# One weighing of v for all eight batches of a gated attention and MLP kernel, with a rewritten instruction list

## The chip, the cores and the metric

The kernel runs on one core of a Trainium2 chip. The metric is the device time of one launch in microseconds; lower is better. All times here are microseconds (us) unless they are marked ns. The engines are TensorE (PE, with its weight loads as PEld), VectorE (DVE), ScalarE (ACT), GpSimd (POOL) and SyncE (SP, which issues DMAs).

## What is computed

Attention over 8 batches, 8 heads, 576 positions and 64 columns a head, with a causal mask and a gate `s` that adds a bias; then a layer norm and an MLP of 512 to 2048 to 512 columns with a residual. The reference, cut to what matters:

```python
scores = scale * np.matmul(q, k.transpose(0, 1, 3, 2))
cum = np.cumsum(np.maximum(s, 0.0), axis=-1)
bias = -(cum[:, :, :, None] - cum[:, :, None, :])
scores = np.where(causal, -1000000000.0, scores + np.minimum(bias, 0.0))
attn = np.exp(scores - np.max(scores, axis=-1, keepdims=True))
attn = attn / (np.sum(attn, axis=-1, keepdims=True) + 1e-09)
attn_out = np.matmul(attn, v)
...
xn = (x - mu) / np.sqrt(var + 1e-06) * g_ln
out = x + np.maximum(xn @ w_ch1, 0.0) @ w_ch2
```

Row i of the bias is -cum[i] + cum[j]. The term in i falls out of the division by the row's sum, so exp(cum[j]), taken relative to a constant, can be multiplied into row j of v and into the column of ones that gives the row's sum.

## The kernel before

A sequence of 576 positions is four tiles of 128 and a tail of 64. The work of a batch is: bring q and k of each head to columns by position (transposes), scores by key tile and exp of them, the causal mask, the product of exp with v and its column of ones, the division by the sums, the layer norm, and the MLP. The MLP of a batch is a queue of units: 16 units `h` of four 512-column products on w1 (`mlp1`, L758) and 16 units `y` of four on w2 (`mlp2`, L776). The eight tails of 64 rows are put in pairs into four more tiles at the end (`mixed_units`, L822).

Nothing is scheduled by a tool: every engine takes its instructions in the order in which the program issues them, and that order is written by hand as a list of words (`PLAN`, L1273), each of which calls one step (`STEPS`) and may name an engine (`:A` ACT, `:D` DVE, `:P` POOL). `u` and `U` take the next MLP unit from the queue, with its relu on ACT or DVE. What stands ahead of the list (loads, memsets) is in its order in the program. DMAs are issued by SP, ACT and POOL; those of POOL convert float32 to bf16 and stand in POOL's list between its own work.

There are three ways of attention in this kernel:

- Batch 0 goes by tiles. `ld_cast_tile` (L178) loads k and q of a tile; `tile_tr` (L939) transposes 8 heads' blocks in two groups `g` of four heads, `tile_evac` (L951) copies them out of PSUM, `tile_scores` (L961) makes scores and adds the causal mask by a product of `ident` with `maskT` (L974), `tile_exp` takes exp on ACT (L983), `tile_pv` (L1012) multiplies with v, `tile_norm` divides. The gate is part of the scores' products: q and k have 68 rows, 64 of data and four for the cumulative sum in three bf16 pieces. These come from a chain at the start: relu, scan (L292), pieces (L303 to L313), transposes of the pieces (`bias_tr`, L271) and copies into the rows of k and q (`bias_cols`, L280). Steps named `T`, `e`, `S`, `x`, `V`, `N` in the list.
- Batch 1 goes by heads: `tr_kind` (L317, six transposes for a pair of heads), `evac_half` (L329), `scores` (L382, one head of 68 rows, masks by a product for the first heads), `scores_d` (L420), `pv` (L573), `pv_norm`. The gate's rows come by SP's DMAs (`aug`, L261).
- Batches 2 to 7 go by pairs of heads: `burst` (L541) makes the scores of two heads at once, one in rows 0 to 63 and one in rows 64 to 127 of TensorE; `burst_exp` (L551); `burst_mask` (L560, POOL); `pv_two` (L613); `norm_two` (L639). The 64-row tails of the eight heads are one step (`tails`, L514). The gate is multiplied into v on POOL (`weigh_v`, L229) with `wt`, the exp of the cumulative sum (`sums_rel`, `sums_tr`, `sums_exp`, L1111 to L1130), and `weigh_ones` (L239) writes wt in two bf16 pieces into the two ones columns, four POOL steps a batch. Batch 2's q and k are loaded by pairs, copied to the side (`side_two`, L342), transposed (`tr_two`, L355) and copied out (`evac_two`); those of batches 3 to 7 are loaded as float32 rows by SP, cast by POOL (`cast_rows`) and transposed by DMA (`tr_rows`).

The early steps use four kinds of PSUM banks: `m` 2, `s` 3, `t` 2, `o` 1. The step `to` (`to_pairs`, L1096) closes these for `m` 2 and `s` 6. `keep_warm` (L851) makes products of zeros, nine at the start and three in the list.

Of the kernel before, what the change touches and what calls it, by code (L numbers as in the profile page):

```python
# [9 lines left out]
F32 = mybir.dt.float32  # L10
# [20 lines left out]
def fast_path(  # L31
# [24 lines left out]
    KA = D + 4  # L56
# [4 lines left out]
    NP = B * NJ  # L61
    NOLD = 2
    NPAIR = 3
    N0 = 12
    D2 = D + 2
    ET = H * TL + 2 * TL
    NM = 10
    KT = 96
# [12 lines left out]
    ps = ctx.enter_context(ExitStack())  # L81
    pool = {
        tag: ps.enter_context(
            tc.tile_pool(name="ps_" + tag, bufs=n, space=bass.MemoryType.PSUM)
        )
        for tag, n in (("m", 2), ("s", 3), ("t", 2), ("o", 1))
    }

    def ptile(tag, shape, name, dtype=F32):
        return pool[tag].tile(shape, dtype, name=name, tag=tag)  # L90
# [5 lines left out]
    maskT = const.tile([P, P], BF16, name="maskT")  # L96
# [8 lines left out]
    eight = hT[0:BH, 0, 0 : 2 * P].bitcast(F32)  # L105
# [6 lines left out]
    def home(gam):  # L112
        return 2 if gam == 2 else gam % 2

# [4 lines left out]
    rinvs = const.tile([P, B, H, NT], F32, name="rinvs")  # L119
    c_end = const.tile([BH, 1], F32, name="c_end")  # L120
# [4 lines left out]
    c3f = const.tile([P, 3 * S], BF16, name="c3")  # L125
    c3 = c3f[0:KT].rearrange("p (j s) -> p j s", j=3)
    ed = [c3f[:, i * ET : (i + 1) * ET] for i in range(2)]
    c_hi, c_mid, c_lo = (c3[0:BH, j, :] for j in range(3))
    zeros = hT[:, 1, :]

    rowb = const.tile([P, NT, 2 * H, KA], BF16, name="rowb")

    rows = [
        x[:, 0 : NT * 2 * H * D].rearrange("p (t u h d) -> p t u h d", t=NT, u=2, h=H)
        for x in (rowb.rearrange("p t h c -> p (t h c)"), kqf[2])
# [29 lines left out]
    def tile_dst(kind, t):  # L165
        pn = P if t < NF else TL
        u = "kq".index(kind)
        return rowb[0:pn, t, u * H : (u + 1) * H, 0:D]
# [16 lines left out]
    def ld_cast_pair(g):  # L185
        ld_cast("k", g)
        ld_cast("q", g)

    def ld_cast_v(b, t):
        pn = P if t < NF else TL  # L190
        nc.gpsimd.dma_start(
            out=v_bf[b % 2][:pn, t, :, 0:D],
            in_=v[b, :, t * P : t * P + pn, :].rearrange("h s d -> s h d"),
        )

# [5 lines left out]
    def ld_f32(kind, b, t):  # L201
        pn = pn_of(t)
        own = kind == "v" and "v" in pool
        tmp = (pool["v"] if own else stage).tile([P, H, D], F32, name="rowtmp", tag="st")
        nc.sync.dma_start(
            out=tmp[0:pn],
            in_=src_of[kind][b, :, t * P : t * P + pn, :].rearrange("h s d -> s h d"),
        )
        loaded[kind, b, t] = tmp

# [28 lines left out]
    def weigh_ones(b, eng="pool"):  # L239
# [21 lines left out]
    def aug(gam, eng, h0=0):  # L261
        r = slice(gam * G + h0, gam * G + G)
        i = home(gam)
        eng.dma_start(out=kq[i][D : D + 1, 1, h0:G, 0:S], in_=c_hi[r, :])
        for j in range(3):
            eng.dma_start(out=kq[i][D + 1 + j : D + 2 + j, 0, h0:G, 0:S], in_=c3[r, j, :])

    trc_bank = ptile("o", [P, 3 * NT * BH + KT - BH], "trc", BF16)
    trc = trc_bank[:, 0 : 3 * NT * BH].rearrange("p (t j x) -> p j t x", t=NT, j=3)

    def bias_tr(t):  # L271
        pn = P if t < NF else TL
        for j in range(3):
            o = (t * 3 + j) * BH
            nc.tensor.transpose(
                trc_bank[0:pn, o : o + KT], c3[:, j, t * P : t * P + pn], ident[0:KT, 0:KT]
            )


    def bias_cols(t0, t1, pn=P):  # L280
        nc.vector.tensor_copy(
            out=rowb[0:pn, t0:t1, 0:H, D + 1 : KA],
            in_=trc[0:pn, :, t0:t1, 0:H].rearrange("p j t x -> p t x j"),
        )
        nc.vector.tensor_copy(out=rowb[0:pn, t0:t1, H : 2 * H, D], in_=trc[0:pn, 0, t0:t1, 0:H])


    def sums_in(c0, c1):
        return (c_first if c1 <= 2 * P else c_in)[:, c0:c1]

    def cum_scan(c0, c1):
        nc.vector.tensor_tensor_scan(  # L292
            out=c_sc[:, c0:c1],
            data0=c_one[:, 0 : c1 - c0],
            data1=sums_in(c0, c1),
            initial=0.0 if c0 == 0 else c_sc[:, c0 - 1 : c0],
            op0=ALU.mult,
            op1=ALU.add,
        )

    def cum_cast(src, dst, c0, c1, eng):  # L303
        x, y = src(c0, c1), dst[:, c0:c1]
        if eng == "act":
            nc.scalar.copy(out=y, in_=x)
        else:
            nc.vector.tensor_tensor(out=y, in0=x, in1=x, op=ALU.max)

    def cum_rest(src, piece, dst, c0, c1):  # L310
        nc.vector.tensor_tensor(
            out=dst(c0, c1), in0=src(c0, c1), in1=piece[:, c0:c1], op=ALU.subtract
        )  # L313

    trs = {}

    def tr_kind(kind, g):  # L317
        src = ready.pop((kind, g))
        tr = ptile("t", [P, S], "trqk", BF16)
        for t in range(QT):  # L320

            nc.tensor.transpose(
                tr[:, t * QP : (t + 1) * QP],
                src[0:QP].rearrange("p h c -> p (h c)")[:, t * P : (t + 1) * P],
                ident[0:QP, 0:QP],
            )
        trs[kind, g] = tr

    def evac_half(kind, g, w, eng):  # L329
        tr, hh = trs[kind, g], (g % 2) * 2  # L330
        dst = kq[home(g // 2)][0:D, "kq".index(kind), hh : hh + 2, 0:S].rearrange(
            "d u (p r w) -> d u p r w", r=QT // 2, w=2
        )
        copy_on(
            eng,
            dst[:, :, :, :, w],
            tr[w * D : (w + 1) * D, :].rearrange("d (u r p) -> d u p r", u=2, p=QP),
        )

    sided = {}  # L340

    def side_two(kind, g, eng):  # L342

        o = (2 * g + "kq".index(kind)) % 4 * 2 * QT * D
        x = rowb.rearrange("p t h c -> p (t h c)")[:, o : o + 2 * QT * D].rearrange(
            "p (t h d) -> p t h d", t=QT, h=2
        )
        copy_on(
            eng,
            x[0:QP],  # L350
            ready.pop((kind, g))[0:QP].rearrange("p h (t d) -> p t h d", t=QT),
        )
        sided[kind, g] = x

    def tr_two(kind, g):  # L355

        src = sided.pop((kind, g))
        tr = ptile("t", [P, QT, QP], "trp", BF16)
        for t in range(QT):
            nc.tensor.transpose(  # L360
                tr[:, t, :], src[0:QP, t].rearrange("p h d -> p (h d)"), ident[0:QP, 0:QP]
            )
        trs[kind, g] = tr
# [12 lines left out]
    def k_cols(b, h, kb):  # L376
        return kq[home(b * 2 + h // G)][0:KA, 0, h % G, kb * P : (kb + 1) * P]

    def q_cols(b, h, q0, q1):
        return [(q0, q1, kq[home(b * 2 + h // G)][0:KA, 1, h % G, q0:q1])]  # L380

    def scores(b, h):  # L382
        e = er[:, h % 4, :]
        pe_mask = b * H + h < NM

        def bank(name, blocks, o):
            a = ptile("s", [P, 512], name)
            for c, kb, q0, q1, diag in blocks:
                for a0, a1, cols in q_cols(b, h, q0, q1):
                    nc.tensor.matmul(  # L390
                        a[:, c + a0 - q0 : c + a1 - q0],
                        lhsT=k_cols(b, h, kb),
                        rhs=cols,
                        start=True,
                        stop=not (pe_mask and diag),
                    )
                if pe_mask and diag:
                    nc.tensor.matmul(
                        a[:, c : c + P], lhsT=ident, rhs=maskT, start=False, stop=True
                    )  # L400
            nc.scalar.activation(out=e[:, o : o + 512], in_=a, func=ACT.Exp, scale=scale)

        bank("sa", ((0, 0, 0, 512, True),), 0)
        bank("sb", ((0, 0, 512, 576, False), (64, 1, 128, 576, True)), OB)
        bank("sc", ((0, 2, 256, 576, True), (320, 3, 384, 576, True)), OC)
        if pe_mask:
            return
        for o, step in ((0, OB + 64), (OC, 320)):
# [11 lines left out]
    def scores_d(b, j):  # L420
# [17 lines left out]
        if pe_mask:  # L438
            return
# [12 lines left out]
    def k_pair(b, j, i, kb):  # L452
        r = slice(i * D, (i + 1) * D)
        if b < NPAIR:
            return kq_flat(b)[r, 0, j, kb * P : (kb + 1) * P]
# [1104 lines left out]
```

## Time and profile before

| what | us |
|---|---|
| three runs | 347.93, 351.93, 352.02 |
| their median | 351.93 |
| the profiled execution | 349.01 |
| its span | 347.3 |
| first MLP product of batch 0 starts | 23.86 |
| first burst of batch 2, of batch 3 starts | 70.17, 97.72 |
| the last products end | 340.9 |

The profile is of one execution. The span goes from the first to the last instruction of the program; 1.7 us of the profiled execution lie around it. A row of TensorE gives its products: stationary rows * columns, then the output's partitions x columns. [...] "Idle before" is the time in which the engine stood still before the rows of a group, with what ended it.

### The profile page before, as it was taken

How to read it: one execution, taken by the hardware profiler on the slowest of the kernel's cores; microseconds unless marked ns; L12 is line 12 of the kernel's file. 1: busy time of each engine (PE TensorE's matmuls, PEld its weight loads, DVE VectorE, ACT ScalarE, POOL GpSimd, SP SyncE). 2: the span in 40 equal slices, each digit the busy share in tenths (PEclk: the TensorE clock that was granted, in tenths of full speed). 3: DMA queues.
4: the chain of work that ended last, by engine and by line, in shares of the span. 5: the costliest groups of instructions: out<-in, count | busy, mean ns of one | idle time of the engine just before them, and what ended most of it. 6: DMA issues, size and time to landing. Idle time of an engine off the chain costs nothing.

```text
span 347.3 us, 8007 instructions
## 1 busy us (share of the span) xinstructions
PE 332.4 (96%) x3066; PEld 186.2 (54%) x3092; DVE 207.8 (60%) x592; ACT 185.4 (53%) x343; POOL 168.7 (49%) x306
## 2 busy tenths in 40 slices
PE   5999999999999999999999999999999999999992
PEld 2898856545545555555555555554555444444452
DVE  6597898937675687456753764557447624514321
ACT  4587889668655686457636864386344104203100
POOL 8898568786577775855684376441201001000000
PEclk9699999999999999999999999999999999999998
DMA  9999999999979999998677955500410221020022
GB/s 157 178 191 180 204 201 211 220 259 202 233 178 191 207 217 178 230 226 168 153 196 180 221 99 143 137 2 2 121 62 0 58 95 45 2 91 31 2 60 69
DMA packets 147486, 48.62 MB, mean 140 GB/s; under 512 B 135185, under 2 KB 142897, under 8 KB 147441
## 3 DMA queue, kind: packets, MB, share of 16 engines
q1 hardware_dynamic: 121616, 38.34, 51.7%
q0 software_dynamic: 24304, 8.92, 21.9%
q10 hardware_dynamic: 1520, 0.79, 0.9%
q8 instruction: 26, 0.43, 0.5%
q14 instruction: 20, 0.16, 0.1%
HBM read 37.11 MB, written 9.44 MB: 134 GB/s over the span
## 4 chain that ended last, share of the span: by engine, by line
PE 88%; DMA 4%; DVE 3%; issue 1%; ACT 1%; POOL 1%; DVEq 0%; ACTq 0%
PE py L780 36%; PE ph L761 32%; PE pot L627 7%; DMA kp<-in_k_dram 3%; PE sa L548 2%; PE trt L944 2%; PE sc L548 2%; PE sb L548 2%; PE ph L1068 1%; DMA hT<-in_s_dram 1%; PE st L966 1%; PE trp L360 1%; PE pot L583 1%; PE pot L1024 1%; DVE c_sc L292 0%
## 5 line engine op out<-in xcount | busy, mean ns | idle before, releaser
L780 PE MATMUL py<-w_bf,hT 128*128 128x512 bf16 (+2 forms) x583 | 128.4, 367 | 2.2 <-DVE yo L792 0.8
L761 PE MATMUL ph<-xT,w_bf 128*128 128x512 bf16 x480 | 109.8, 379 | 0.0
L752 ACT ACTIVATE hT<-ph 128x512 bf16<-128x512 f32 x97 | 58.1, 603 | 80.8 <-PE ph L761 79.4
L780 PEld LDWEIGHTS <-hT 128*128 128x128 bf16 x608 | 56.1, 98 | 62.0 <-issue 1.3
L761 PEld LDWEIGHTS <-w_bf 128*128 128x128 bf16 x544 | 51.0, 98 | 56.3
L492 POOL TENSOR_SCALAR_AFFINE_SELECT er<-er 128x256 bf16<-128x256 bf16 x96 | 38.8, 418 | 62.0 <-ACT er L553 46.9
L792 DVE SCALAR_TENSOR_TENSOR yo<-py,rstd,xb 128x512 f32<-128x512 f32 x32 | 24.0, 751 | 48.7 <-PE py L780 41.0
L750 DVE TENSOR_SCALAR hT<-ph 128x512 bf16<-128x512 f32 x39 | 26.8, 691 | 26.8 <-PE ph L761 26.0
L553 ACT ACTIVATE er<-sb 128x512 bf16<-128x512 f32 x48 | 28.1, 607 | 21.1 <-PE sb L548 14.3
L553 ACT ACTIVATE er<-sa 128x512 bf16<-128x512 f32 x48 | 28.6, 607 | 13.7 <-PE sa L548 12.4
L232 POOL TENSOR_TENSOR v_bf<-rowtmp,wt 128x512 bf16<-128x512 f32 (+1 forms) x30 | 33.1, 1110 | 2.0 <-DMA rowtmp<-in_v_dram 1.9
L553 ACT ACTIVATE er<-sc 128x512 bf16<-128x512 f32 x48 | 28.6, 611 | 4.1 <-PE sc L548 4.1
L627 PEld LDWEIGHTS <-er 128*128 128x128 bf16 x672 | 25.7, 97 | 9.5 <-issue 0.6
L627 PE MATMUL pot<-v_bf,er 128*128 128x66 bf16 x672 | 28.0, 193 | 0.1
L684 POOL TENSOR_TENSOR rstd<-rstd,mhalf 128x4 f32<-128x4 f32 (+1 forms) x8 | 8.8, 1099 | 38.0 <-DVE rstd L683 34.4
L644 DVE TENSOR_REDUCE sums<-pot 128x5 f32<-128x10 f32 x48 | 8.0, 166 | 30.4 <-PE pot L627 30.1
L710 DVE SCALAR_TENSOR_TENSOR xn<-xb,mv,gb 128x512 bf16<-128x512 f32 x28 | 25.1, 895 | 1.0
L669 DVE BATCH_NORM_STATS2 stats<-xb 128x6 f32<-128x128 f32 (+1 forms) x84 | 23.8, 323 | 0.4
L217 POOL CAST kq<-rowtmp 128x512 bf16<-128x512 f32 (+1 forms) x30 | 19.6, 662 | 8.4 <-DMA rowtmp<-in_k_dram 7.5
L647 DVE TENSOR_TENSOR xb<-pot,rinvs 128x256 f32<-128x256 f32 x48 | 20.4, 425 | 1.6
L548 PEld LDWEIGHTS <-kq 64*128 64x128 bf16 x360 | 11.2, 94 | 10.1 <-issue 4.7
L983 ACT ACTIVATE er<-st 128x512 bf16<-128x512 f32 x24 | 13.1, 603 | 4.2 <-PE st L974 2.8
(169 smaller groups left out, 396.6 us busy)
## 6 DMA issues: line engine op xcount, KB each, us to landing
out_dram<-yo SPq DMA_DIRECT2D x32, 256.0 KB
rowtmp<-in_v_dram SPq DMA_DIRECT2D x24, 256.0 KB
rowtmp<-in_k_dram SPq DMA_DIRECT2D x20, 256.0 KB
rowtmp<-in_q_dram SPq DMA_DIRECT2D x20, 256.0 KB
w_bf<-in_moe_w_ch_dram POOLq DMA_DIRECT2D x8, 512.0 KB, 7.9
kp<-in_k_dram POOLq DMA_DIRECT2D x8, 144.0 KB, 8.5
qp<-in_q_dram POOLq DMA_DIRECT2D x8, 144.0 KB, 8.5
v_bf<-in_v_dram POOLq DMA_DIRECT2D x8, 128.0 KB, 7.2
```

The costliest lines, as they stand in the source:

```text
L232: e.tensor_tensor(out=v_bf[b % 2][0:pn, t, :, 0:D], in0=loaded.pop(("v", b, t))[0:pn], in1=wt[0:pn, t, b, :].unsqueeze(2).to_broadcast([pn ...
L492: nc.gpsimd.affine_select(out=out, in_=out, compare_op=ALU.is_ge, fill=0.0, base=0, pattern=pattern, channel_multiplier=-1,)
L548: nc.tensor.matmul(a, lhsT=lhsT, rhs=rhs, start=True, stop=True)
L553: nc.scalar.activation(out=er[:, 2 * n % 4 + i, o : o + 512], in_=bank["B", n].pop((name, i)), func=ACT.Exp, scale=scale,)
L627: nc.tensor.matmul(pot[:, t, :], lhsT=cols, rhs=v_bf[b % 2][:, kb, h, :], start=(kb == 0), stop=(kb == t),)
L669: nc.vector.bn_stats(out=st[b][:, t, part, :], in_=x_tiles(b)[t][:, lo:hi])
L710: nc.vector.scalar_tensor_tensor(out=xn, in0=tiles[t], scalar=mvs[b][:, t, 0:1] if b > 0 else mean0[:, t : t + 1], in1=gb, op0=ALU.subtrac ...
L750: nc.vector.tensor_scalar_max(out=dst, in0=ph, scalar1=0.0)
L752: nc.scalar.activation(out=dst, in_=ph, func=ACT.Relu)
L761: nc.tensor.matmul(ph, lhsT=w1_bf[:, kd, fb * P : (fb + 1) * P], rhs=xT[:, :, kd, :], start=(kd == 0), stop=(kd == KD - 1),)
L780: nc.tensor.matmul(py[t], lhsT=hT[:, fb, t * P : (t + 1) * P], rhs=w2_bf[:, fb, c0:c1], start=(fb == 0), stop=(fb == FB - 1),)
L792: nc.vector.scalar_tensor_tensor(out=yo, in0=py[t], scalar=rs, in1=x[:, c0:c1], op0=ALU.mult, op1=ALU.add)
```

## The change

The gate's rows in q and k are gone, and with them batch 0's and batch 1's own ways through scores and v. All eight batches multiply the gate into v and the ones columns.

- Batch 0 still goes by tiles, but its transposes take two heads of 64 columns together (eight products a tile for all heads), its scores are made for two heads at once in the two halves of the rows, and the causal mask is set after exp: by POOL's select or by a minimum with `upper` on DVE. Its tail goes by `tails`. Its v is loaded as float32 by SP and weighed.
- Batch 1 goes by pairs of heads as batches 2 to 7 do. Its v is loaded as float32 and weighed too.
- `tr_two` no longer reads a side copy: each of the six transposes of a pair becomes two, one a head, each of which writes 64 partitions. `side_two`, `tr_kind` and `evac_half` are gone.
- The ones columns of all batches are made in one step (`wo`), and a copy of one batch's share goes to v's buffer (`vo`).
- Weighings (`vm`) and copies of ones may go to DVE as well as POOL.
- The scan of the gate is one instruction of 576 columns. The relu no longer multiplies by 8, and the exp of the sums no longer scales.
- PSUM has `m` 2 and `s` 6 from the start. `to` only gives the pair buffers over to v.
- `hold` takes three of the eight float32 staging buffers out of use, and `let_go` gives one back.
- `keep_warm(20)` at the start takes the place of nine products of zeros and three later ones. A word of the list may carry a count (`3*S.0.0`), for so many products of zeros ahead of its first tile; no word in the list has one.
- Loads and memsets that stood ahead of the list are words of it, and the list has a new order throughout. MLP units of batch 0 are taken in plain order.

The diff, cut to its core:

```diff
-        for tag, n in (("m", 2), ("s", 3), ("t", 2), ("o", 1))
+        for tag, n in (("m", 2), ("s", 6))
...
+    def hold(n):
+        for _ in range(n):
+            x = stage.tile([P, H, D], F32, name="held", tag="st")
+            nc.vector.memset(x[0:1, 0, 0:8], 0.0)
+            held.append(x)
...
+    def ones_all(eng):
         e = nc.vector if eng == "dve" else nc.gpsimd
         for pn, ts_ in ((P, slice(0, NF)), (TL, slice(NF, NT))):
-            one = v_bf[b % 2][0:pn, ts_, :, D:D2]
-            w = wt[0:pn, ts_, b, :]
-            e.tensor_copy(out=one[:, :, :, 0], in_=w)
-            e.tensor_tensor(out=one[:, :, :, 1], in0=w, in1=one[:, :, :, 0], op=ALU.subtract)
+            w = wt[0:pn, ts_]
+            hi, lo = (wo[0:pn, ts_, :, :, i] for i in range(2))
+            e.tensor_copy(out=hi, in_=w)
+            e.tensor_tensor(out=lo, in0=w, in1=hi, op=ALU.subtract)
+
+    def weigh_ones(b, eng):
+        copy_on(eng, v_bf[b % 2][:, :, :, D:D2], wo[:, :, b])
...
     def tr_two(kind, g):
-        src = sided.pop((kind, g))
-        tr = ptile("t", [P, QT, QP], "trp", BF16)
+        src = ready.pop((kind, g))
+        tr = ptile("s", [P, QT, QP], "trp", BF16)
         for t in range(QT):
-            nc.tensor.transpose(
-                tr[:, t, :], src[0:QP, t].rearrange("p h d -> p (h d)"), ident[0:QP, 0:QP]
-            )
+            for h in range(2):
+                nc.tensor.transpose(
+                    tr[h * D : (h + 1) * D, t, :],
+                    src[0:QP, h, t * D : (t + 1) * D],
+                    ident[0:QP, 0:QP],
+                )
...
-    nc.sync.dma_start(out=c_first, in_=s_rows[:, 0 : 2 * P])
     ld_tile("q", 0, nc.scalar)
     ld_tile("k", 0, nc.sync)
-    nc.sync.dma_start(out=c_in[:, 2 * P : S], in_=s_rows[:, 2 * P : S])
+    nc.sync.dma_start(out=c_in, in_=s.rearrange("b h s -> (b h) s"))
...
-    keep_warm(9)
+    keep_warm(20)
...
+    def tile_tr(t):
+        pn = pn_of(t)
+        tr = ptile("s", [P, 2 * NJ, P], "trt", BF16)
+        x = rowb[0:pn, t].rearrange("p u (j i) d -> p (u j) (i d)", i=2)
+        for c in range(2 * NJ):
+            nc.tensor.transpose(tr[:, c, 0:pn], x[:, c], ident[0:pn, 0:pn])
...
+    def tile_scores(t, i):
+        two = [ptile("s", [P, 512], "st") for _ in range(2)]
+        w = pn_of(t)
+        for c in range(512 // w):
             hh, kb = divmod(4 * i + c, t + 1) if t < NF else (c // 2, 2 * i + c % 2)
...
+            for g in range(2):
+                r = slice(g * D, (g + 1) * D)
                 nc.tensor.matmul(
-                    a[:, c * P : (c + 1) * P], lhsT=ident, rhs=maskT, start=False, stop=True
+                    two[g][:, c * w : (c + 1) * w],
+                    lhsT=kqf[0][r, tile_cols(kb, 0, hh, P)],
+                    rhs=kqf[0][r, tile_cols(t, 1, hh, w)],
+                    start=True,
+                    stop=True,
                 )
...
+    def tile_mask(t, g, eng):
+        at = [block_at(t, g, hh * (t + 1) + t) for hh in range(G)]
...
+            if eng == "dve":
+                nc.vector.tensor_tensor(
+                    out=two, in0=two, in1=upper.unsqueeze(1).to_broadcast([P, n, P]), op=ALU.min
+                )
+            else:
+                select(two, [[0, n], [1, P]])
...
-        + queue[8:16]
-        + [queue[16 + 4 * u + qr] for qr in range(4) for u in range(2)]
-        + queue[24:]
+        + queue[8:]
```

The first words of the new list, up to the first MLP product of batch 0 (`M.0.1.0`), and the place of the first burst of batch 1 (`B2.4`):

```
c.k:A lt.q.1 id lt.k.1 c.q:A T.0 z8.1:D ho.3 rl:A qu.1 e.0.1:A e.0.0:A S.0.0 lv.0.0 lv.0.1 zo:D
lt.k.2 z1:D sc wr T.1 zr:P zi wT e.1.1:D x.0.0.0 e.1.0:A S.1.1 S.1.0 lv.0.2 lt.q.2 mk lv.0.3
x.0.1.0 lt.k.4 qu.2 lt.k.3 lt.q.3 z8.0:P lv.0.4 wx wo:D vo.0:D vm.0.0:D x.1.1.1 T.2 lv.1.0
k.0.1:D V.0.1 k.0.0:P V.0.0 x.1.1.0 k.1.1:P z7.1:D x.1.0.0 x.1.0.1 e.2.0:A gb e.2.1:A S.2.0
vm.0.1:P lv.1.1 lv.1.2 vm.0.2:D lt.q.4 lv.1.3 lv.1.4 N.0.0 lv.2.0 S.2.1 V.1.1 x.2.0.1 hc x.2.0.0
x.2.1.0 S.2.2 x.2.1.2 k.1.0:P lg.k.5 T.3 e.3.0:A N.0.1 zk:D z7.0:P x.2.0.2 N.1.1 x.2.1.1 e.3.1:D
V.1.0 S.3.2 w1.0 S.3.1 lg.q.5 N.1.0 L.0 L.1 x.3.0.1 lg.k.4 x.3.0.2 S.3.3 x.3.0.3 k.2.0:P k.2.1:D
lg.k.6 x.3.1.1 T.4 B.1.0 e.4.0:A e.4.1:A lg.k.7 lg.q.4 B.1.1 z6:P S.3.0 V.2.0 V.2.1 S.4.0 N.2.0
X.1 w1.1 N.2.1 tk.0 x.3.1.3 x.3.1.0 x.3.1.2 k.3.1:P x.3.0.0 y.1:D x.4.1.0 x.4.0.0 lg.q.6 sd.0
F.k.5 se.0 L.2 sm.0 X.0 S.4.1 x.4.1.1 G.k.5:A lg.q.7 M.0.1.0 M.0.1.1
...
X.3 y.3:D lg.q.10 se.1 B2.4 bx.4.0 B.3.0 N.4.0 B.0.0
```

`lt` loads and casts a tile of k or q, `lg` a pair of heads, `lv` a tile of v, `w1` and `w2` a quarter of a weight; `c` casts tile 0; `sc`, `wr`, `wT`, `wx` are the scan, the sums relative to the reference point, their transposes and their exp; `vm` weighs a tile of v; `k` sets the causal mask.

More of the change, by code (lines that the diff above doesn't have):

```diff
@@ L320, in tr_kind @@
         for t in range(QT):
[L322 to L338, printed above, removed]
@@ L374, in kq_flat @@
         return kqf[b % 2].rearrange("p (u j s) -> p u j s", u=2, j=NJ)
[L376 to L408, printed above, removed]
-            two = e[:, o : o + 2 * step].rearrange("p (i c) -> p i c", c=step)[:, :, 0:P]
-            nc.gpsimd.affine_select(
-                out=two,
-                in_=two,
-                compare_op=ALU.is_ge,
-                fill=0.0,
-                base=0,
-                pattern=[[0, 2], [1, P]],
-                channel_multiplier=-1,
-            )
@@ L1250, in fast_path @@
         "sm": tails_mask,
+        "B2": burst,
         "bx": burst_exp,
```

629 lines of the change are left out of this document (200 added, 429 removed).

## The prediction

> **What bounds the kernel now.** I read the page first, then the busy time in six stretches that I cut at list words, then TensorE's groups by form, its timeline around one two-head and one one-head step, and the chain of waits. Page, parts 1 and 2:
>
> ```profile
> span 347.3 us, 8007 instructions
> ...
> PE 332.4 (96%) x3066; PEld 186.2 (54%) x3092; DVE 207.8 (60%) x592; ACT 185.4 (53%) x343; POOL 168.7 (49%) x306
> ...
> PE   5999999999999999999999999999999999999992
> ...
> PEclk9699999999999999999999999999999999999998
> ```
>
> TensorE is full in 38 of 40 slices, so outside the opening the time is its list of products. The stretches (columns: busy time and count by engine, granted clock, DMA share, GB/s) end at 23.86, where the first MLP product of batch 0 (`M.0.1.0`) starts; at 70.17 (first burst of batch 2); at 97.72 (first burst of batch 3, `B2.12`):
>
> ```profile
> 0.00:7.00 7.00, 4.25 (x13) 1.52 (x13) 4.36 (x18) 2.94 (x6) 6.09 (x14) 1.00 0.96 146
> 7.00:14.00 7.00, 5.43 (x49) 5.05 (x50) 4.33 (x14) 3.77 (x8) 6.14 (x8) 0.52 2.33 173
> 14.00:23.86 9.86, 9.49 (x181) 8.97 (x179) 8.08 (x29) 8.54 (x17) 9.45 (x18) 0.99 1.63 193
> 23.86:70.17 46.31, 44.64 (x651) 32.52 (x651) 40.45 (x100) 38.62 (x70) 34.90 (x59) 1.00 1.32 204
> 70.17:97.72 27.55, 26.65 (x266) 13.98 (x266) 16.30 (x54) 19.46 (x37) 18.97 (x37) 1.00 1.14 226
> 97.72:347.30 249.58, 241.98 (x1922) 124.16 (x1942) 134.29 (x382) 112.07 (x208) 93.12 (x174) 1.00 0.52 115
> ```
>
> The opening has TensorE waiting, and at half clock from 7 to 14; POOL is its busiest engine (21.7 of 23.86). After that nothing waits for long. A record's length is no price, since products overlap; I price by starts. Chain in order of time:
>
> ```profile
> 120.35 0.91 PE pot L627 x30
> ...
> 285.35 13.81 PE ph L761 x64
> ```
>
> A 512-column product takes 13.81/64 = 0.216, a product with v 0.91/30 = 0.030. TensorE's timeline, one head (68 rows) and then two heads at once (64 rows each):
>
> ```profile
> 56.33 0.38 PE L390 MATMUL sa<-kq 68*128 68x512 bf16 x1
> ...
> 56.98 1.03 PE L780 MATMUL py<-w_bf,hT 128*128 128x512 bf16 x3
> 57.85 0.42 PE L360 MATMUL trp<-ident,rowb 96*128 96x96 bf16 x6
> 58.10 0.62 PE L583 MATMUL pot<-v_bf,er 128*128 128x65 bf16 x15
> ...
> 82.27 0.39 PE L548 MATMUL sa<-kq 64*128 64x512 bf16 x2
> 82.49 0.38 PE L548 MATMUL sb<-kq 64*128 64x64 bf16 x4
> ...
> 83.02 0.60 PE L627 MATMUL pot<-v_bf,er 128*128 128x66 bf16 x14
> ```
>
> From start to next start: 0.65 for one head's scores, 0.75 for two, since their two 512-column products take 0.22 together; 0.25 for the six transposes of a pair. Last, ACT's exps of batch 0 and the weights' row among the page's DMA issues (us to landing at its end):
>
> ```profile
> L983 ACT ACTIVATE er<-st 128x512 bf16<-128x512 f32 x24 | 13.1, 603 | 4.2 <-PE st L974 2.8
> ...
> w_bf<-in_moe_w_ch_dram POOLq DMA_DIRECT2D x8, 512.0 KB, 7.9
> ```
>
> **The change, step by step.** I counted each list's products and priced them so. After `B2.12` both lists hold the same 241.5 us. Before it, the old list has 81.6: 11.9 ahead of `M.0.1.0` and 69.7 between, which took 97.72 - 23.86 = 73.9 (4.2 of waits). The new one has 74.7: 7.8 ahead and 66.9 between. The 6.9 less:
> - Batch 0's tile transposes: 5 of 8 products in place of 10 (8 at 128 columns run from 15.47 to 15.91, 0.44): -2.2. The 15 gate transposes at 0.042: -0.6.
> - Its scores: 24 steps with 32 mask products plus a last one, 7.8, become 12 steps of 16 products or 8 pairs. A pair runs in the time of one product, as the 0.22 shows, so a step of eight pairs with 512 columns in all costs 0.22: 2.7 together, with up to 0.11 each for the gap that the timeline has at a burst's end. -5.1, at worst -3.8. The tails' step adds 0.2.
> - Batch 1's scores: eight heads at 0.65 and their masks, 6.1, become four bursts at 0.77 and a tails step, 3.3: -2.7.
> - Products with v have 66 columns: +0.1. Three products of zeros inside the old list: -0.65.
> - The 16 pair transposes (batches 1 and 2) go from 6 to 12 products of 96 columns, each to half of the partitions: 16 x 0.255 = 4.1 before, and 8.2 at 12 x 0.042, which the 74.7 holds. No product of before writes to half of the partitions. If two overlap, as score pairs do, a step stays at 0.25; if not, and the burst's gaps come on top at both ends (0.80 less 1536 columns at 0.216 for 512, 0.15), 0.67. I take 0.46, the middle, as both rows are equally near: 15 of them lie after `M.0.1.0`, -0.7 against 66.9 (from -3.9 to +2.4).
>
> [...]
>
> Off TensorE's path in the dense part: eight rowb copies (0.83 each on ACT) and 16 half copies (0.80, seven on ACT) go, eight full copies (0.64, ACT) come; SP loses eight gate rows (0.6 to 0.76 an issue); DVE gets a sum (0.17) per norm. Cover: 44.64 of TensorE against 40.45 DVE and 38.62 ACT in that stretch; without it the ACT copies would gain 7. Ones columns: six times four POOL steps (0.33 + 0.29 + 0.34 + 0.23) become four wide DVE steps (0.35 to 0.6 each by the nearest tensor rows) and eight small copies; POOL is under half busy there, so 0, and the DVE steps lie in the opening. Counted zeros ahead of a tile: no list word carries a count, so 0. Guard: two more 0.22 us DVE products, hidden.
>
> **The opening.** Gone: relu, scan, splits and bias columns ahead of the first transpose (8.30). New: 20 products of zeros; six at 0.427 (half clock) and 14 at 0.216 from 1.27 end at 6.9, so the first transposes start at 6.9, 1.4 sooner. But batch 0 now needs weights for v, masks after exp, and all its exps but one ahead of `M.0.1.0` (23; the old list had 16).
> - ACT, in list order: two casts 0.61, relu 0.7 (0.47 for 320 columns), six copies of 512 at 0.60, two of 256 at 0.35, 22 exps at 0.525 (eight took 4.20), the gate exp 0.45: 18.2 up to the exp whose bank `M.0.1.0` takes over. It starts at 4.5 (first cast 4.76 before), waits about 1.1 for the zeros' end and the transposes, 0.6 for the first scores and 1.1 for tile 2's, which stand behind tile 1's products with v: 25.5.
> - DVE: scan 1.6, gate 1.2, ones 1.4, two weighings 0.8 each, six norms at 0.85, masks and stages: some 17 from 6.0, so 23.
> - POOL: the first w1 quarter, issued at 11.68 before, now stands behind eight tile loads (0.87), two masks of tile 1, one of tile 0, a weighing (1.13) and zeros: 13.9 us of steps from 0.6 and some 3.8 of waiting for exps (tile 1's are done near 12.5), so 18.3; landing 7.8 later as before, 26.1. Queued behind it: the pairs of batch 1 and w1's other quarters.
> - DMA: q, k, v of batch 0, s, the gains and one pair at 0.55 to 0.9 each, as they landed between 7.6 and 24, then the quarter at 2.5: 20.0. The first loads of batch 3, early in SP's old list, come later.
>
> Moved with this: the ten casting loads of v of batches 0 and 1 leave POOL's queue (0.87 each) and become float32 loads on SP (0.6 an issue) and ten weighings (1.13 on POOL, about 0.8 on DVE). Three of the eight stage buffers are held at first, so SP stops at batch 1's first v load until a weighing frees a buffer; behind it stand only more v loads. Batch 3's row loads, casts and DMA transposes come later too: the last transpose stands 4.4 us of products ahead of `B2.12`, 9.7 before; SP has nothing older to wait for there, so 0, and up to 3 if it lands late. The second MLP's first tiles need all quarters of w2 in turn; the last is due at about 55 and issued near 42: hidden.
>
> So `M.0.1.0` at 26.0, 2.1 later than before, with 2.8 less work left. Bounds: 22.8 (ACT without a wait) and 29 (each engine's waits doubled).
>
> **Sum.** 26.0 + 66.9 - 0.7 + 3.0 of waits (old list 4.2; DMA has less to do before batch 2; ends 1 and 7) = 95.2 against 97.72: -2.5. From there nothing differs in work. Span 344.8; the profiled execution, 349.01 for a span of 347.3, becomes 346.5. The three runs (347.93, 351.93, 352.02) average 350.6 and their median is 2.9 over the profiled one; I take their mean, 350.6 - 2.5: **348**. Ends: 22.8 + 66.9 - 3.9 + 1 = 86.8, -10.9; 29 + 66.9 + 2.4 + 7 = 105.3, +7.6.
>
> **Rivals.** 2% (7 us) is about what a measurement of this kernel can tell from no change.
> - *The opening is not held by ACT and POOL, and the transposes overlap:* then TensorE's list decides: `M.0.1.0` near 23, 3.9 less, waits as small as 1.5: about -10, 340.5. For it: the PE row; against: 18.2 us of ACT's own work ahead of it. 0.22.
> - *Slower: the first w1 quarter waits in POOL's list.* Every us after 18.3 at its issue delays `M.0.1.0`; past 21 the kernel is slower than before, and an issue at 29.5, if each mask and weighing waits for its own exp and load in turn, lands at 37: +11, 359. For it: POOL was busiest in the opening; against: no POOL wait over 0.7 us in the old opening. 0.16.
> - *The clock is low when the dense part begins.* 7.8 us of products in 19 us leave TensorE under half busy from 6.9 on. The old opening shows 0.52 over 7 us after such idling; the same stretch after 26 would cost 3.4: 351.5. 0.12.
>
> [...]
>
> **Chances.** Forecast 0.50 (own range 343 to 353), the others 0.22, 0.16, 0.12. Faster by over 2% (below 344.9): 0.06 of the forecast and 0.19 of the first rival, 0.25. Slower (over 359): 0.02, 0.11 of the second, 0.01 of the third, 0.14. Same 0.61. Range 340 to 357: it cuts half of the first rival and over half of the second.
>
> **What would show it.** `M.0.1.0` (first 128-column product on w1) near 26, with ACT busy nearly throughout from 7 to 26; the first w1 quarter landing near 26; pair transposes at 0.4 to 0.5 a step; the mask rows of TensorE gone; the first burst of batch 3 near 95; clock 1.00 after 27. Wrong if that burst starts under 90 or over 100, or if TensorE waits after it.

## The result, and the profile after

The changed kernel takes 355.13 us (median of 11 runs, 352.57 to 355.86) against 351.21 of the kernel before (11 runs beside it, 347.93 to 352.5): a ratio of 1.0124, 95% interval 1.0096 to 1.0152. It is 4 us slower where 348, 2.5 us less, was forecast; 355.13 lies inside the range, on the wrong side. The profiled execution has a span of 353.9, 6.6 over that of before (347.3), and the chip ran it at a mean clock of 0.973. Page, parts 1 and 2:

```profile
span 353.9 us, 8001 instructions
...
PE 334.8 (95%) x3091; PEld 179.9 (51%) x3091; DVE 215.3 (61%) x611; ACT 178.9 (51%) x333; POOL 156.7 (44%) x273
...
PE   8479999998999999799999999999999999999993
...
PEclk9957999999999999989999999999999999999998
```

TensorE now has weak places in the opening, in the slice from 80 to 88 us (8) and in that from 142 to 150 (7), with a lower clock in the slice behind it (8 in the row of the clock). The stretches, cut at the first transpose (8.33), at the fall of the clock, at the first MLP product of batch 0 (29.89) and at the first bursts of batches 2 and 3 (67.09 and 99.12); columns as before:

```profile
8.33:17.08 8.75, 3.75 (x64) 2.80 (x64) 5.71 (x15) 6.01 (x12) 4.72 (x8) 1.00 1.85 174
17.08:29.89 12.81, 10.94 (x174) 8.99 (x173) 10.49 (x41) 9.84 (x20) 10.55 (x19) 0.50 1.28 196
29.89:67.09 37.20, 37.09 (x622) 25.57 (x618) 29.38 (x90) 28.22 (x52) 26.64 (x45) 0.99 1.18 200
67.09:99.12 32.03, 30.39 (x282) 15.65 (x282) 20.91 (x65) 21.58 (x40) 23.39 (x38) 1.00 1.03 194
99.12:353.87 254.75, 245.60 (x1943) 124.21 (x1942) 146.47 (x396) 109.90 (x204) 84.39 (x151) 0.99 0.59 121
```

Against before: the opening ends at 29.89 (23.86 before, 26.0 forecast). The dense part to `B2.12` takes 99.12 - 29.89 = 69.23, and the forecast said 66.9 - 0.7 + 3.0 = 69.2. From `B2.12` to the end it takes 254.75 instead of 249.58: 5.2 us are lost where the forecast has nothing. So 353.87 is 344.8 plus 3.9 in the opening plus 5.2 behind `B2.12`.

The largest loss behind `B2.12`, in TensorE's timeline (start, length, what, idle before):

```profile
142.69 3.19 PE L579 MATMUL py<-w_bf,hT 128*128 128x512 bf16 x14
...
146.26 0.39 PE L387 MATMUL sc<-kq 64*128 64x256 bf16 x8
149.27 0.58 PE L427 MATMUL pot<-v_bf,er 128*128 128x66 bf16 x14 [2.63 <-POOL v_bf L230]
149.69 0.19 PE L427 MATMUL pot<-v_bf,ed 128*128 128x66 bf16 x1
149.72 5.30 PE L579 MATMUL py<-w_bf,hT 128*128 128x512 bf16 x16
```

TensorE stands for 2.63 us, and then 16 products of 512 columns take 5.30, since the clock is at 0.50 from 150.2 to 153.6: another 1.7 us (at full clock, in run 6, the same 16 take 3.62). The profile names a weighing of v on POOL, but that row ends at 149.26 and writes v of batch 5, while the product is of batch 4. VectorE's timeline shows a step that ends at the same time and that the product does depend on:

```profile
141.65 0.75 DVE L591 SCALAR_TENSOR_TENSOR yo<-py,rstd,xb 128x512 f32<-128x512 f32 x1 [2.08 <-PE py L579]
145.00 2.44 DVE L230 TENSOR_TENSOR v_bf<-rowtmp,wt 128x512 bf16<-128x512 f32 x1 [2.59 <-DMA rowtmp<-in_v_dram]
147.36 0.22 DVE L487 BATCH_NORM_AGGREGATE mv<-stats 128x2 f32<-128x18 f32 x1
147.61 0.75 DVE L510 SCALAR_TENSOR_TENSOR xn<-xb,mv,gb 128x512 bf16<-128x512 f32 x1
148.28 0.29 DVE L469 BATCH_NORM_STATS2 stats<-xm 128x6 f32<-128x128 f32 x1
148.49 0.73 DVE L591 SCALAR_TENSOR_TENSOR yo<-py,rstd,xb 128x512 f32<-128x512 f32 x1
```

The word `vm.5.3:D` put a weighing of batch 5 on VectorE. It waits 2.59 us for its v row, takes 2.44 (0.67 at 119.21, with no POOL step beside it), and three norm steps and the copy-out `yo` of an MLP tile stand behind it. `yo` ends at 149.22 and frees one of the two `m` banks; a product with v takes such a bank, and this one starts at 149.27. In runs 3 and 4, too, this product starts 0.05 after that `yo`, at other times. Runs 5 and 6 test this reading. The kernel before has all weighings on POOL (a row of its page: busy time, mean ns of one, and POOL's idle time before them):

```profile
L232 POOL TENSOR_TENSOR v_bf<-rowtmp,wt 128x512 bf16<-128x512 f32 (+1 forms) x30 | 33.1, 1110 | 2.0 <-DMA rowtmp<-in_v_dram 1.9
```

The new list has 17 on VectorE, 13 of them in batches 2 to 7.

### The profile page after: what moved, and what is told of

Read it like the earlier page. It is cut to its first block, busy times and chain, and to the rows that moved or that the text cites. A ratio compares the mean times of both kernels' runs of the same rounds, so it can differ in the third digit from the quotient of the medians.

```text
span 353.9 us, 8001 instructions
## 1 busy us (share of the span) xinstructions
PE 334.8 (95%) x3091; PEld 179.9 (51%) x3091; DVE 215.3 (61%) x611; ACT 178.9 (51%) x333; POOL 156.7 (44%) x273
## 2 busy tenths in 40 slices
DMA packets 147340, 49.76 MB, mean 141 GB/s; under 512 B 135136, under 2 KB 142688, under 8 KB 147296
## 4 chain that ended last, share of the span: by engine, by line
PE 76%; POOL 7%; DMA 6%; DVE 3%; issue 3%; ACT 2%; SPq 1%; POOLq 0%; DVEq 0%
PE py L579 29%; PE ph L560 29%; PE pot L427 6%; DMA rowtmp<-in_q_dram 3%; POOL kq L215 2%; PE ph L813 2%; DMA rowb<-in_q_dram 2%; PE idle L653 2%; POOL er L331 2%; POOL v_bf L230 2%; PE sa L387 2%; SPq L192 1%; PE sc L387 1%; PE sb L387 1%; PE pot L769 1%
## 5 line engine op out<-in xcount | busy, mean ns | idle before, releaser
L579 PE MATMUL py<-w_bf,hT 128*128 128x512 bf16 (+2 forms) x608 | 132.6, 371 | 0.0
L331 POOL TENSOR_SCALAR_AFFINE_SELECT er<-er 128x256 bf16<-128x256 bf16 (+1 forms) x119 | 51.5, 452 | 71.2 <-ACT er L392 64.7
L392 ACT ACTIVATE er<-sa 128x512 bf16<-128x512 f32 x56 | 33.3, 607 | 23.8 <-PE sa L387 17.9
L392 ACT ACTIVATE er<-sb 128x512 bf16<-128x512 f32 x56 | 33.0, 606 | 17.1 <-PE pot L427 11.6
L392 ACT ACTIVATE er<-sc 128x512 bf16<-128x512 f32 x56 | 33.2, 611 | 12.3 <-PE pot L427 6.6
L427 PEld LDWEIGHTS <-er 128*128 128x128 bf16 x784 | 29.9, 97 | 16.9 <-POOL er L331 4.6
L427 PE MATMUL pot<-v_bf,er 128*128 128x66 bf16 x784 | 33.1, 193 | 4.8 <-POOL v_bf L230 2.6
L230 POOL TENSOR_TENSOR v_bf<-rowtmp,wt 128x512 bf16<-128x512 f32 (+1 forms) x23 | 26.2, 1148 | 4.8 <-DMA rowtmp<-in_v_dram 4.6
L447 DVE TENSOR_TENSOR xb<-pot,rinvs 128x256 f32<-128x256 f32 x56 | 23.8, 424 | 1.9
L230 DVE TENSOR_TENSOR v_bf<-rowtmp,wt 128x512 bf16<-128x512 f32 (+1 forms) x17 | 18.0, 1059 | 3.5 <-DMA rowtmp<-in_v_dram 3.3
```

The costliest lines, as they stand in the source:

```text
L230: e.tensor_tensor(out=v_bf[b % 2][0:pn, t, :, 0:D], in0=loaded.pop(("v", b, t))[0:pn], in1=wt[0:pn, t, b, :].unsqueeze(2).to_broadcast([pn ...
L331: nc.gpsimd.affine_select(out=out, in_=out, compare_op=ALU.is_ge, fill=0.0, base=0, pattern=pattern, channel_multiplier=-1,)
L392: nc.scalar.activation(out=er[:, 2 * n % 4 + i, o : o + 512], in_=bank["B", n].pop((name, i)), func=ACT.Exp, scale=scale,)
L427: nc.tensor.matmul(pot[:, t, :], lhsT=cols, rhs=v_bf[b % 2][:, kb, h, :], start=(kb == 0), stop=(kb == t),)
L579: nc.tensor.matmul(py[t], lhsT=hT[:, fb, t * P : (t + 1) * P], rhs=w2_bf[:, fb, c0:c1], start=(fb == 0), stop=(fb == FB - 1),)
```

## The experiments

**1. The new list to `B2.12`, the old order behind it.**

```
  ... lr.4.3 vm.3.4:P ga.2.0.0 u u u lv.4.0 B2.12        (new list)
- bx.12.2 bx.12.4 ga.2.2.1 ... (new order)
+ cr.4.0.1 cr.4.1.1 lr.4.4 lv.4.1 ga.2.1.0 bx.12.0 U bx.12.4 bm.12.2 ... (old order)
```

> The changed kernel's list up to the first burst of batch 3 (B2.12), the list of before from there on; both leave the same 247 MLP units and nearly the same other words, so only the order (and the engine of the weighings) behind B2.12 is changed. Order theory (the new list's back part is the worse one): the wait of 2.8 us at 146 and the half clock behind it go, B2.20 comes 60.3 us after B2.12 as in the trace of before (61.7 there, 66.5 after the change), and of the 355.1 some 5 go: 350. Loads theory (the rows of batches 4 and 5 are late because DMA is full from the opening on, whatever the order): waits of 2 us or more stay between 99 and 166: 353 to 356. Opening and clock theories: the back part is no cause, 355.

Measured: 355.07, ratio 1.0137 (1.0067 to 1.0207). The wait at 146 shrank to 1.4, but TensorE waited 3.1 at 116 for the DMA transpose of batch 2's normalised x, and `B2.20` came 66.8 after `B2.12`. The order theory fell: the old order, put behind this front, loses as much at another place. Behind `B2.12` it also has all its weighings on POOL, so taking them off VectorE is not enough in every order.

**2. POOL's loads of the opening ahead of its masks.**

```
- ... V.0.1 k.0.0:P V.0.0 ... gb ... lt.q.4 ... lg.k.5 ... w1.0
+ ... V.0.1 lt.q.4 w1.0 gb lg.k.5 k.0.0:P V.0.0 ...
```

> In POOL's list of the opening the loads of q's tail tile, of the first w1 quarter, of the gains and of one pair are moved ahead of the first masks, so that POOL issues them from 9 on and not between 14.6 and 19.3. Opening theory: the first MLP product of batch 0 (29.89 after the change) starts at 26 to 27, the first burst of batch 3 at 96 (99.12), and the time falls by 3: 352. Order theory: the start moves as much, but the back part waits for its own order, and half or more of it is lost by 160: 353.5 to 355. Clock theory: with TensorE at half clock to 30.7 the first MLP product comes at 28 at best, 353.5.

Measured: 355.86, ratio 1.0138 (1.0071 to 1.0206). The first w1 quarter landed at 22.5 instead of 28.7, and the first MLP product still started at 29.91: from 24.5 on TensorE ran up to it without a wait over 0.25, as after the change. So the second rival of the prediction (the quarter stuck in POOL's list) was not what held the opening. The wait at 146 stayed too (3.2 at 147.5, and the half clock behind it).

**3. 45 products of zeros in TensorE's gaps of the opening.**

```
- S.0.0 ... S.1.1 ... V.0.1 ... V.1.1 ... S.3.2 ... T.4
+ 5*S.0.0 ... 3*S.1.1 ... 24*V.0.1 ... 6*V.1.1 ... 4*S.3.2 ... 3*T.4
```

> 45 products of zeros (4.9 us at full clock) stand in six of TensorE's gaps between 8.7 and 24, and nothing else is changed. Clock theory: the clock stays at 1.00 from 7 to 30, TensorE's work between 23.7 and 29.9 takes 3 us less, the first MLP product starts at 27 and the time falls by 3: 352. Opening theory: the first w1 quarter lands at 28.7 whatever the clock, so the first MLP product moves by at most 1.2: 354. Order theory: 354 to 355.

Measured: 352.61, ratio 1.0062 (1.0029 to 1.0096). The clock stayed at 1.00 and the first MLP product came at 27.69, 2.2 sooner (0.3 of it because the first transposes started at 8.01 and not 8.33). But `B2.12` was only 0.6 sooner (98.53): TensorE waited 0.9 for a pair's row at 29, 0.8 for a weights' quarter at 58 and 1.1 for a DMA transpose at 78 instead. The rest of the gain is at 146, where TensorE's wait fell to 0.2: the v row of batch 5 landed at 143.4 instead of 145.0, and the weighing and `yo` behind it came as much sooner. The size was as the clock theory said, the place was not.

**4. No held stage buffers.**

```
- ... z8.1:D ho.3 rl:A ... x.2.0.1 hc x.2.0.0 ... se.2 hc u u ... bm.10.0 hc lr.4.0 ...
+ ... z8.1:D rl:A ... x.2.0.1 x.2.0.0 ... se.2 u u ... bm.10.0 lr.4.0 ...
```

> The three stage buffers are never held, so SP issues batch 1's v loads from 8 on instead of 15 to 19, and rows of batch 3 ahead of 60. Theory of held buffers: DMA moves the later rows earlier, the waits for rows at 86, 88 and 146 shrink, and the time falls by 2 to 4: 351 to 353. Opening theory: the v loads come ahead of q's tail tile and the w1 quarter in the queues, the first MLP product starts at 31 or later, 356. Order theory: 355.

Measured: 353.61, ratio 1.0074 (1.0028 to 1.0119). `B2.12` 1.2 sooner (97.89), so the held buffers cost about that. The wait at 146 stayed, 2.8 from 145.25 on, but the clock did not fall behind it.

**5. The weighings of batches 2 to 7 on POOL.**

```
- vm.3.0:D vm.2.3:D vm.3.3:D vm.4.0:D vm.4.1:D vm.4.4:D vm.5.3:D vm.5.2:D vm.5.0:D vm.6.3:D vm.6.4:D vm.6.0:D vm.7.1:D
+ the same 13 words, each with :P, at their places
```

> The 13 weighings of v of batches 2 to 7 that the changed kernel makes on DVE go to POOL, at the same places of the list. VectorE theory (a weighing on DVE waits for its v row and then for POOL, and holds back the copy-out of an MLP tile that TensorE's next bank waits for): DVE never stands behind a v row again, the 2.8 us at 146 and the half clock behind it go; POOL gets 13 x 1.05 us more, and its masks stand behind the rows instead, which gives part of it back: 351.5 to 353. Loads theory: POOL's list waits for the same rows, so the masks come later and TensorE waits as long as before: 355 or more.

Measured: 351.35, ratio 1.0024 (0.9985 to 1.0062), which can't be told from the kernel before. TensorE, then VectorE, at the same place:

```profile
145.68 0.39 PE L387 MATMUL sc<-kq 64*128 64x256 bf16 x8
146.00 0.59 PE L427 MATMUL pot<-v_bf,er 128*128 128x66 bf16 x14
146.44 0.19 PE L427 MATMUL pot<-v_bf,ed 128*128 128x66 bf16 x1
146.46 2.75 PE L579 MATMUL py<-w_bf,hT 128*128 128x512 bf16 x12
```

```profile
142.68 0.29 DVE L469 BATCH_NORM_STATS2 stats<-xm 128x6 f32<-128x128 f32 x1
144.48 0.75 DVE L591 SCALAR_TENSOR_TENSOR yo<-py,rstd,xb 128x512 f32<-128x512 f32 x1 [1.51 <-PE py L579]
```

`yo` now waits for TensorE and not TensorE for `yo`; the wait and the half clock are gone (`B2.20` at 160.99 instead of 165.63). POOL's 13 more steps, 1.04 each, stand ahead of masks, and TensorE waits 1.1 for a mask at 77 and 0.9 at 116 (0.8 each at 86 and 88 after the change).

**6. One weighing moved.**

```
- ... tk.5 lr.6.0 vm.5.3:D bx.18.4 ... B2.19 Y.17.0 bx.19.2 vm.5.2:D
+ ... tk.5 lr.6.0 bx.18.4 ... B2.19 Y.17.0 bx.19.2 vm.5.3:D vm.5.2:D
```

> One word moved: the weighing of row tile 3 of batch 5 on DVE (vm.5.3) stands behind the first product with v of head pair 17 instead of some ten MLP units ahead of it. VectorE theory: the copy-out of the MLP tile no longer stands behind it, TensorE's wait at 146.5 shrinks from 2.8 to the 1.2 that POOL's last mask of that pair needs (done at 147.7), the clock stays full, and the time falls by 3: 352. Loads theory (POOL's casts behind late rows are what holds TensorE): TensorE still stands until 149, 355.

Measured: 352.08, ratio 1.0045 (1.0008 to 1.0082). TensorE:

```profile
146.36 0.32 PE L427 MATMUL pot<-v_bf,er 128*128 128x66 bf16 x5
147.63 0.45 PE L427 MATMUL pot<-v_bf,er 128*128 128x66 bf16 x9 [0.95 <-POOL er L331]
```

The product begins at once and then waits 0.95 for POOL's mask, as expected, and the clock stays at 1.00 there. One word of the list's 1,289 carries 3 of the 4 us. POOL's casts behind late rows are the next wait in line, 1 us.

**7. Four of eight heads of v's rows of batches 2 to 5.** The other half of v's values there is left out; the weighing (not shown) reads the loaded half twice.

```
+ nh = H // 2 if kind == "v" and 2 <= b <= 5 else H
- out=tmp[0:pn], in_=src_of[kind][b, :, ...]
+ out=tmp[0:pn, 0:nh], in_=src_of[kind][b, 0:nh, ...]
```

> Of the v rows of batches 2 to 5 only four of the eight heads are loaded, and the weighing uses them for both halves, so half of v's values there are left out (2.4 MB, some 11 us of transfer at the 210 GB/s of these stretches); the engines do the same work. Loads theory (DMA is the second bound up to 200): the waits at 86, 88, 115 and 146 and the half clock go, 350. VectorE theory: the row for vm.5.3 lands earlier too, so the wait at 146 goes with it, but a weighing on DVE beside POOL still takes 1.5 to 2.9 us: 350.5 to 352. If DMA is no bound, nothing changes: 355.

Measured: 349.50, ratio 0.996 (0.9927 to 0.9993). No wait over 0.9 is left behind 75 us. At the critical place the row is there in time:

```profile
139.79 0.68 DVE L232 TENSOR_TENSOR v_bf<-rowtmp,wt 128x512 bf16<-128x512 f32 x1
```

So the weighing on VectorE hurts because its row is late (and then takes 2.44 beside POOL's steps), and the row is late behind the other loads: after the change SP issues 18 row loads between 121.8 and 141.5, one in 1.16 us, and from 110 to 140 the queues are busy at a share of 1.18 and more and move 212 to 223 GB/s. Both theories predicted this run; only the fifth and sixth tell them apart.

**8. Four moves together** (2, 3, 4 and 6).

> The moves of three earlier runs and the one of the run before last together: POOL's loads of the opening ahead of its masks, the 45 products of zeros, no held buffers, and vm.5.3 later. Clock theory of the opening: with the clock at 1.00 and the first w1 quarter at 22.5, the first MLP product comes near 26.5 (27.69 with zeros alone, where the quarter landed at 27.63), batch 3's first burst at 96.5; VectorE theory: no wait over 1 us behind it. Together 97 + 250.5 of the rest and 1.7 around the span: 349, at or just under the kernel of before. If the gains overlap (each only moves TensorE up to the same late rows), 352.

Measured: 351.72, ratio 1.0022 (0.9988 to 1.0057). Behind batch 2 no wait is over 0.6, as expected. But the first MLP product came at 28.81 and `B2.8` at 69.69, 2.6 later than after the change: with the quarter ahead of them the gains landed at 23.4 (19.6 after the change), VectorE waited 1.7 for them, and TensorE 1.5 for the mask behind, at 24. At 32 it waited 1.9 for a weighing that took 3.91 on VectorE (from 29.73 on) while POOL issued DMAs and weighed three tiles, and the clock was at 0.50 from 35.80 to 39.21.

**9. The zeros, and the 13 weighings on POOL** (3 and 5).

> The 45 products of zeros of the clock run and, of the run with the weighings, all 13 of batches 2 to 7 on POOL. If the two causes are separate (clock and w1 quarter ahead of the first MLP product, weighings on VectorE behind batch 3's first burst), the gains add: the first MLP product at 27.7, batch 3's first burst at 96.5 to 98.3, B2.20 62.5 behind it, 350 to 350.5. If both only move TensorE up to the same late rows, 351.5.

Measured: 351.65, ratio 1.0024 (0.9989 to 1.0058). The gains do not add. The first MLP product was 2.5 sooner than in run 5 (27.39 against 29.85), `B2.12` only 0.4 (97.90 against 98.33): waits of 0.4 for a pair at 29 and 0.5 for a w1 quarter at 35, which run 5 does not have, took part of it. The rest is not traced to single waits.

**10. Fewer weighings moved, and some loads and a mask of the opening sooner.**

```
- wx wo:D vo.0:D vm.0.0:D ... k.0.1:D ... gb ... vm.0.1:P ... lt.q.4 ... w1.0
+ wx k.0.1:D wo:D vo.0:D vm.0.0:D ... vm.0.1:P lt.q.4 w1.0 gb ...
- vm.4.0:D vm.4.1:D vm.4.4:D vm.5.3:D vm.5.2:D vm.5.0:D
+ the same six with :P; zeros as in run 3
```

> The zeros, only the six weighings of batches 4 and 5 on POOL, and in the opening the loads of q's tail tile, the first w1 quarter and the gains ahead of two of POOL's later steps, and one mask on DVE ahead of the ones columns. Opening theory (with the clock up, the w1 quarter, landed at 27.63 of 27.69 with zeros alone, is what the first MLP product waits for): that product starts at 25.5 to 26.5, batch 3's first burst at 97, and the time is 349 to 349.5. If DMA only passes the wait on (what comes ahead delays k, v and the pairs behind it), the first MLP product is at 27 or later and the rest of the list waits for pairs: 351.

Measured: 355.38, ratio 1.0135 (1.0085 to 1.0185); the first MLP product at 32.55. The w1 quarter landed at 24.5, but the gains, now issued 3 us later, at 26.0, and VectorE's list stood behind them (VectorE, then TensorE):

```profile
26.12 0.84 DVE L510 SCALAR_TENSOR_TENSOR xn<-xb,mean,gb 128x512 bf16<-128x512 f32 x1 [4.39 <-DMA gb<-in_moe_g_ln_dram]
```

```profile
28.47 0.73 PE L769 MATMUL pot<-v_bf,er 128*128 128x66 bf16 x10 [4.38 <-DVE er L747]
```

A mask of tile 2 on VectorE was queued behind that normalisation. It is the same fault as at 146, made by the experiment itself; the clock fell behind this wait too (0.50 from 27.20 to 34.03).

**11. Run 9 with four of eight heads of v's rows of batches 0 and 1.** The lines of run 7, with `b <= 1`; the other half of v's values there is left out.

> The kernel with the zeros and the weighings on POOL, and of the v rows of batches 0 and 1 only four of eight heads are loaded (the weighing uses them for both halves, so half of v's values there are left out): 0.6 MB less, 2.8 us of transfer at 210 GB/s, half of what the change added to DMA. Loads theory (between the first MLP product and batch 2 TensorE waits for pairs and w1 quarters, so that 2.5 us won in the opening shrank to 0.4 at B2.12): the quarters and pairs land some 2 us earlier, B2.8 starts at 64 to 64.5 (66.21 with all rows), B2.12 at 95.5 to 96, and 349.5 are left of 351.65. Rival (what lies there is TensorE's own work): B2.12 at 97.5 or later, 351.5.

Measured: 350.77, ratio 0.9992 (0.9961 to 1.0023). The w1 quarters landed 0.9 to 1.8 sooner, and the waits for a pair and a quarter are gone, but `B2.8` was at 66.47 and `B2.12` at 98.43, no sooner than in run 9. The profiled execution has a TensorE wait of 1.4 at 36 that the profile can put down to nothing ("issue"); without it `B2.8` would be at 65.1, as it is in run 12. So these rows are worth some 1 us here, half of what the loads theory said, though 1.2 MB were left out (49.76 less 48.58) and not the 0.6 of the expectation. The times alone (350.77, and 351.65 in run 9) do not show it: the two intervals overlap.

**12. Run 9 with four of eight heads of v's rows of batches 0 to 5.** The same with `b <= 5`.

> The same with half of the v rows of batches 0 to 5, 3.5 MB less (half of v's values there are left out). Loads theory: besides B2.12 at 95.5, the waits of 1.0 to 1.1 us at 77 and 116 go, since POOL's casts and weighings wait less, and the time is 347: what is left of the change once DMA is no bound, some 4 under the kernel of before. Rival (DMA is no bound any more after the weighings are on POOL): 351.

Measured: 349.07, ratio 0.995 (0.9921 to 0.9979); `B2.12` at 96.77, 349 instead of the 347 expected. The waits at 76 and 115 stayed at 1.1 and 0.9, so these are not made by the half of v's rows that is left out.

## Why the prediction was wrong, step by step

- **TensorE's work: right in kind, and the sum by luck.** 69.23 from the first MLP product to `B2.12` against 69.2. Pair transposes took 0.35 to 0.38 a step ahead of other work and 0.26 to 0.28 ahead of another such step, against 0.46 (bounds 0.25 and 0.67). The 12 products of a step start 22 ns apart in the mean: the two column halves (one a head) 3 or 4 ns apart, the next two mostly 39 or 40 ns later. A product of full width took 42 ns before, so these column halves overlap:

```profile
33.60 0.45 PE L271 MATMUL trp<-ident,kp 96*64 96x96 bf16 x12
33.98 0.62 PE L813 MATMUL ph<-xT,w_bf 128*128 128x128 bf16 x8
```

  The 15 steps took 5.1 where the sum has 6.9. So 4.9 are left besides the products as they were priced, where the sum has 3.0 of waits; about 0.4 of it is the half clock up to 30.74.

- **"From there nothing differs in work": the step that failed.** The work is the same, and the waits are not. The step priced weighings on VectorE only in the opening, at 0.8 each; the new list's `:D` on 13 later ones was in the diff and was given neither a row to wait for nor a count of what is queued behind it. Runs 5 and 6 show 3 to 4 us of the 5.2 there. The list of what would make it wrong did name the sign, a wait of TensorE after that burst, but no mechanism. The rest, 1.3 in run 5 (a tail of 250.87 against 249.58), is mostly the 0.9 at 116 behind POOL's masks.
- **"DMA has less to do before batch 2": right in bytes, and no help.** 19.0 MB moved up to `B2.12` against 19.8 before. But v of batches 0 and 1 lands as float32, which is 1.1 MB more in all (49.76 MB, 48.62 before), so 30.7 MB instead of 28.8 lie behind `B2.12`, and from 110 to 140 the queues are busier (a share of 1.19 against 1.09). Halving the rows of batches 0 and 1 is worth 1 us at `B2.8` (runs 11 and 12), but with the queues at that share the row of `vm.5.3` landed at 145.0, and with half of the rows it was there by 139.8 (run 7); behind the late row stood three norm steps and `yo`.
- **`M.0.1.0` at 26.0: 3.9 too early.** POOL's issue of the first w1 quarter was near the forecast (19.31 against 18.3), its landing later (28.70 against 26.1), and neither mattered (run 2). Two other terms did:
  - The zeros: the forecast has six of the 20 products at 0.427 and their end at 6.9. In this execution 13 start 0.427 apart, and the first transposes start at 8.33, 1.4 late:

```profile
1.27 7.23 PE L653 MATMUL idle<-hT 128*128 128x512 bf16 x20 [1.27 <-DVE warm L667]
8.33 0.61 PE L688 MATMUL trt<-ident,rowb 128*128 128x128 bf16 x8
```

  (The row of the granted clock has 1.00 there; the starts show the lower pace.) Where the pace changes differs from execution to execution: at 6.79 here, between 4.57 and 6.76 in runs 1 to 12, and the first transposes start anywhere from 7.16 to 8.33.
  - From the first transposes to `M.0.1.0` the forecast has 19.1. It took 21.6 after the change and 21.7 to 22.2 in the runs without added zeros (1, 2, 4 to 7), whatever the start, and 19.7 to 19.9 in those with the zeros of run 3 and no other move in the opening (3, 9, 11, 12). So the half clock made some 1.8 of the 3.9 (21.6 less 19.8), and 0.7 is left open. It came ahead of the dense part (17.08 to 30.74), where the third rival had put it behind 26.

  ACT, which the forecast took for the bound, was busy 15.85 of the 21.56 us from 8.33 on. TensorE's largest wait there is 3.4 at 13, for a mask on VectorE behind ones columns and a weighing; 3.03 of it fill the 3.41 us ahead of the fall of the clock. In run 12, at full clock, the chain that ended last is VectorE's for 11.3 of the 15.0 us from 12.75 to 27.76. Whether that mask can come sooner, run 10 does not show, since its gains came late.
- **What 2 us there are worth: little.** In run 9 the first MLP product is 2.5 sooner and `B2.12` 0.4; a start forecast from the opening must be followed to the loads behind it.

The half clocks after the change, up to the last products, lasted 13.65 (17.08 to 30.74) and 3.41 (150.20 to 153.62), the first four times as long as the second; and 17.08 less three times 3.41 is 6.84, where the pace of the zeros changes (6.79).

## What to carry to other kernels

Before a step is put on another engine, look at what it waits for and what is queued behind it there: a step of 0.7 us that waits for a DMA costs what stands behind it in an in-order list, here a copy-out that frees TensorE's bank. Where the profile names a releaser that the data flow doesn't have, look for another engine whose step ends within 0.1 us of the same time, and test by moving that one word. Time won early is only worth what the next late load leaves of it.

## What the runs showed of the hardware

**VectorE's weighing beside POOL's steps.** Three of the 17 after the change had no POOL step beside them and took 0.63, 0.67 and 0.68; the 14 others took 0.67 to 2.89. The longest, and one with no POOL step beside it (VectorE, then POOL):

```profile
114.09 2.89 DVE L230 TENSOR_TENSOR v_bf<-rowtmp,wt 128x512 bf16<-128x512 f32 x1
...
119.21 0.67 DVE L230 TENSOR_TENSOR v_bf<-rowtmp,wt 128x512 bf16<-128x512 f32 x1
```

```profile
114.19 1.16 POOL L215 CAST rowb<-rowtmp 128x512 bf16<-128x512 f32 x2
115.31 1.12 POOL L331 TENSOR_SCALAR_AFFINE_SELECT er<-er 128x256 bf16<-128x256 bf16 x3
116.39 0.70 POOL L142 COPY v_bf<-wo 128x80 bf16<-128x80 bf16 x1
```

The long one ended 0.59 after POOL's copy had begun. The two casts and three selects ahead of that copy took 0.60 and 0.40 each (the medians of such steps are 0.61 and 0.41); the copy took 0.70, where the median is 0.26. From these lengths the author's reading is that the weighing stood through the five steps and ran beside the sixth; what holds it no run here shows. The view of the tile `v_bf` shows the spread that a mean hides:

```profile
L230 POOL TENSOR_TENSOR v_bf<-rowtmp,wt x23: 1034/1045/1593, 15.2 to 223.1; 128x512 bf16<-128x512 f32 x18, 64x512 bf16<-64x512 f32 x5
L230 DVE TENSOR_TENSOR v_bf<-rowtmp,wt x17: 628/801/2892, 14.3 to 227.3; 128x512 bf16<-128x512 f32 x14, 64x512 bf16<-64x512 f32 x3
```

(min, median, max in ns.) The forecast's 0.8 a weighing is the median here; the long ones cost the time.

**Waits ahead of a half clock.** In the traces of before and after the granted clock changes on a grid of 3.41 us: at 7.33, 14.16 and 345.25 before, at 17.08, 30.74, 150.20, 153.62 and 351.59 after, in each trace whole multiples of 3.41 apart. In the dense part a wait with 2.48 of its 2.63 us in one window of that grid (146.79 to 150.20, after the change) was followed by a clock of 0.50 in the next window, as was one of 3.24 with 2.48 in one window (run 2). One of 2.80 that a window's edge cut into 0.78 and 2.01 (run 4), and one of 3.09 cut into 1.71 and 1.38 (run 1), were not. So of waits of nearly the same length (2.63 and 2.80) one cost 1.7 us more, half a per cent of the kernel's time, and the other did not; that this hangs on where a wait lies in the grid is the author's estimate from these four. Idle time alone does not decide it: in the openings windows with 1.7 and 2.0 us of idle (up to 11.30 in run 7 and 35.80 in run 8) were followed by the half clock too. What else counts, no run here separates.
